# Eight PSUM banks, one written-out order: the same steps of an RWKV attention and squared-ReLU MLP kernel in another sequence

## The chip, the cores and the metric

The kernel runs on one core of a Trainium2 chip. A core has five engines with a queue of instructions each: TensorE (PE: matmuls; its weight loads are listed apart as PEld), VectorE (DVE), ScalarE (ACT), GpSimd (POOL) and SyncE (SP, which here only issues DMAs). The metric is the device time of one execution in microseconds.

## What is computed

A linear attention with a decaying state (4 batches, 8 heads, 768 tokens, head size 48), whose output feeds a two-layer MLP with squared ReLU (384 to 2048 to 384).

```python
def _attn_ref(r, k, v, w, u) -> np.ndarray:
    B, H, S, D = r.shape
    state = np.zeros((B, H, D, D), dtype=np.float32)
...
    for t in range(S):
...
        cur = np.einsum('bhd,bhe->bhde', u[None] * kt, vt)
        y[:, :, t] = np.einsum('bhd,bhde->bhe', rt, state + cur)
        state = w[None, :, :, None] * state + np.einsum('bhd,bhe->bhde', kt, vt)
...
def _moe_ref(x, w_in, w_out) -> np.ndarray:
    h = np.maximum(x @ w_in, 0.0)
    return (h * h @ w_out).astype(np.float32)
```

## The kernel before

The 3072 tokens are cut into 24 units of 128 tokens (`UNITS`: batch and chunk). Within a unit the attention is a masked matrix product, and the 48 x 48 state is carried from chunk to chunk of a batch. The MLP runs on groups of one or two units (`GROUPS`).

Nothing is scheduled by a tool while the kernel is built. The text `ORDER` (line 23) lists all 948 steps. Its entries read `name.indices:engine/slot`: `F1.1.2:P/5` is step F1 of group 1, part 2, on TensorE, with PSUM bank 5. The loop at the end goes through the text, notes the slot as the place of the tile that the step writes, and calls the method of that name of class `Do`. Every engine works through its own steps strictly in the order of the text; between engines, semaphores hold a step back until its inputs are there and its slot is free. The order between entries of different engines in the text therefore means nothing by itself, but a step that waits holds up everything behind it on its engine, and on SP and POOL also the DMAs that are issued behind it.

The steps, with their letters for the engines (A = ACT, D = DVE, G = POOL, P = TensorE, S = SP) and the lines at which the profile lists them:

- Setting up: w, u, wc load the decay vectors; lw takes the logarithm; Z (L564) multiplies an identity by itself for nothing but to occupy TensorE (of n matmuls, n/4 are 512 columns wide, the rest 128); bw (L276) spreads the logarithms over the partitions; Wk (L298) and Wt (L302) make the decay factors; mP and mJ the masks; V (L331) and W (L334) load the quarters of the two MLP matrices, from POOL's queue.
- Loading: lp (L325) loads r, k or v of two units at once for the first four units, ld (L321) of one unit for the others.
- Attention on DVE and POOL: kh (L337) and rh (L340) multiply k and r by their factors; P0 (L343), P1 (L347), du (L350) and dv (L355) make the term with u; vb (L253 on ACT, L255 on DVE or POOL, shared with all plain copies) converts v.
- Transposing k and r: for the first four units TK and TR (L364) with the copies KC and RC; for units 4, 5 and 9 T (L398) with the copy Tc; for the others XB (L404), a DMA transpose.
- Attention on TensorE: Ap (L384) or A (L411), masked into SBUF by Bp (L392) or Bm (L419); Y (L428, L436, L440 for the first four units, L450 and L452 later) makes the output of a unit; U (L463) its contribution to the state.
- State: S0 (L478), ts (L481) and S (L484) update the state of a batch, which Y of the batch's next chunk reads: S.18 writes what Y.22 reads.
- Turning the output round: xs (L475) brings Y out of PSUM, then either X (L489), three transposes on TensorE, with the copy xTc, or xX (L496), a DMA transpose on SP's queue.
- MLP: F1 (L505) is a part of the first product, re (L515 ACT, L517 DVE) its ReLU, sq (L522, L524) the square; F2 (L533) adds a quarter of the second product for a unit, os (L253, L255) copies it out, out (L583, L585) stores it. The last unit, 23, has its second product in two column halves: Fh (L547), oh, outh (L560).

V.2 is the third quarter of the first MLP matrix; F1.0.2, F1.1.2 and all F1 of later groups that fall into that quarter wait for it.

The buffers are fixed in number (`POOLS`); PSUM has eight banks of 128 x 512 float32, used by all TensorE steps:

```python
    banks = [psum.tile([128, 512], FP32, name=f"bank_{j}") for j in range(8)]
```

Of the kernel before, what the change touches and what calls it, by code (L numbers as in the profile page):

```python
# [38 lines left out]
F2.1.2:P/7 P1.5:G du.5:D/0 Bm.5.1:D/2 xs.4:D/4 U.4:P/5 sq.2.0:A/11 sq.2.5:A/12 X.4:P/3 Bm.5.0:D/3 Y.5:P/0 re.2.6:D/1
dv.5:G F2.1.0:P/7 sq.2.3:D/13 F2.3.0:P/6 sq.2.6:D/14 xs.5:D/0 X.5:P/4 F2.0.0:P/1 xTc.5:D/1 xTc.4:A/1 F1.3.1:P/0  # L40
ld.k.6:S/6 re.2.2:D/5 sq.2.2:D/15 re.3.1:D/4 ld.r.6:S/6 P0.6:G/0 F1.3.2:P/4 F1.3.6:P/3 ld.v.6:S/6 vb.6:A/6 U.5:P/2
S0.5:D os.1:A/0 F2.3.2:P/6 F2.3.3:P/6 re.3.2:D/3 re.3.6:A/0 sq.3.6:A/16 rh.6:G/6 F2.3.1:P/6 kh.6:G/6 U.6:P/0
sq.3.2:D/17 ld.r.7:S/7 os.0:D/1 S0.4:D F1.3.0:P/2 F1.3.7:P/7 F2.2.3:P/4 re.3.7:A/2 ld.k.7:S/7 ts.6:D/0 kh.7:G/0
os.3:D/2 rh.7:G/0 re.3.0:A/1 F1.3.3:P/3 sq.3.0:A/18 F2.2.2:P/4 F1.3.4:P/1 re.3.3:A/5 sq.3.3:A/19 F2.2.0:P/4 P0.7:G/2
F2.2.1:P/4 os.2:A/3 out.2:A P1.6:G ld.k.8:S/0 P1.7:D ld.k.9:S/1 ld.v.7:S/7 kh.9:D/1 F2.5.1:P/5 S.3:D ld.r.9:S/0
rh.9:G/1 T.9:P/7 P0.9:D/3 sq.3.1:D/20 ld.r.8:S/1 re.3.4:D/0 XB.7:S/0 du.6:D/1 A.7:P/0/6 du.7:D/2 P1.9:G F1.3.5:P/2
Bm.7.1:D/4 F2.4.1:P/3 Bm.7.0:D/5 rh.8:G/2 ld.v.9:S/0 XB.6:S/6 A.6:P/4/1 Bm.6.0:D/6 F2.4.0:P/3 Bm.6.1:D/7 vb.7:A/7
dv.6:G P0.8:G/4 dv.7:G Y.7:P/6 re.3.5:A/3 du.9:D/3 xs.7:D/1 sq.3.7:A/21 F2.4.3:P/3 sq.3.5:A/22 sq.3.4:A/23 out.1:A
Y.6:P/0 U.7:P/4 F2.4.2:P/3 X.7:P/1 F2.5.2:P/5 xTc.7:A/2 Tc.9:A/1 xs.6:D/2 X.6:P/2 os.4:A/3 xTc.6:D/2 ld.r.11:S/2
rh.11:G/3 ld.k.11:S/2 F2.5.0:P/5 ld.r.10:S/3 F1.4.7:P/6 F2.5.3:P/5 kh.8:D/2 kh.11:G/3 P1.8:G ld.k.10:S/3 ts.7:D/1  # L50
ld.v.8:S/1 rh.10:G/4 kh.10:D/4 vb.9:A/0 re.4.7:D/1 sq.4.7:D/24 os.5:A/0 F1.4.1:P/1 re.4.1:A/5 sq.4.1:A/25 F1.4.4:P/7
F1.4.3:P/0 re.4.4:A/4 S.7:G vb.8:G/1 S.6:D du.8:D/4 dv.8:G F1.4.0:P/3 re.4.0:A/2 U.8:P/2 ts.8:D/1 U.9:P/4 F1.4.2:P/6
re.4.3:A/3 XB.11:S/2 A.11:P/5/1 ts.9:D/0 P0.11:G/1 re.4.2:A/0 sq.4.3:A/26 Bm.11.0:D/0 A.9:P/7/3 Bm.9.0:D/1 P0.10:G/0
# [5 lines left out]
xs.11:D/1 ld.r.13:S/5 rh.13:G/0 kh.13:D/0 F1.5.5:P/7 re.5.3:A/3 sq.5.3:A/0 re.5.5:A/0 ld.k.15:S/6 kh.15:G/6 F1.5.7:P/6
F1.5.1:P/3 re.5.7:A/2 F1.5.2:P/1 vb.12:A/4 X.10:P/0 re.5.1:D/1 X.11:P/7 xTc.11:D/1 F1.5.4:P/6 xTc.10:A/1 ld.r.12:S/6  # L60
P0.12:D/2 P1.12:G re.5.0:A/4 rh.12:G/5 P0.15:D/3 du.12:D/1 P1.15:G ld.r.14:S/7 F1.6.2:P/3 out.5:S ld.v.15:S/6
rh.14:G/1 ld.r.17:S/0 F1.5.6:P/7 re.5.6:D/5 F1.6.0:P/0 F1.6.3:P/5 F2.7.1:P/2 F2.6.2:P/4 rh.17:G/2 F2.7.3:P/2 dv.12:G
sq.5.7:A/3 re.5.4:A/3 P0.13:D/4 P1.13:G sq.5.1:A/1 re.6.2:A/2 XB.13:S/0 ld.k.14:S/7 kh.14:G/1 sq.5.5:A/2 F1.6.7:P/7
# [10 lines left out]
rh.16:G/4 dv.15:G F1.7.3:P/0 xs.15:D/0 os.8:D/0 dv.14:G xs.14:D/4 kh.16:D/4 F1.7.7:P/7 S.15:D ld.r.19:S/2 re.7.7:A/5
ld.r.21:S/3 F1.7.0:P/2 rh.19:G/5 sq.7.7:A/16 F1.7.1:P/4 re.7.1:A/2 xX.15:S/0 F1.7.5:P/1 F1.7.2:P/3 P0.16:D/2 P1.16:G
X.14:P/5 xTc.14:D/0 ld.r.18:S/6 re.7.2:A/1 sq.7.1:A/21 re.7.5:A/4 P0.21:D/4 kh.19:G/5 P1.21:G ld.v.17:S/0 re.7.3:A/3
sq.7.2:A/4 P0.19:D/3 S.12:D rh.21:G/3 out.9:S sq.7.3:A/25 ld.k.18:S/4 U.14:P/7 ts.14:D/1 F2.11.2:P/6 F2.11.3:P/6
F1.8.6:P/4 re.8.6:D/0 P0.18:D/1 vb.17:A/0 re.7.0:A/5 XB.16:S/2 out.8:A F1.8.3:P/5 F1.8.7:P/3 re.8.7:D/2 sq.7.5:A/26
# [557 lines left out]
```

## Time and profile before

| | us |
|---|---|
| median of 3 timed runs | 171.6 |
| lowest and highest | 170.86, 171.61 |
| the profiled execution | 169.91 |
| its span, first to last instruction | 168.2 |
| TensorE busy in it | 161.5 |
| DVE busy | 135.3 |
| POOL busy | 104.3 |
| ACT busy | 100.8 |

The profile is of one execution. Rows of instructions have a start, a duration, the engine, the line, output and inputs and a count; a bracket tells how long the engine was idle before and what ended that. Rows of the chain of waits have a start, a duration and what the end of the kernel waited for in that time. A matmul's end is modelled, so busy time of TensorE can hold a stall.

### The profile page before, as it was taken

How to read it: one execution, taken by the hardware profiler on the slowest of the kernel's cores; microseconds unless marked ns; L12 is line 12 of the kernel's file. 1: busy time of each engine (PE TensorE's matmuls, PEld its weight loads, DVE VectorE, ACT ScalarE, POOL GpSimd, SP SyncE). 2: the span in 40 equal slices, each digit the busy share in tenths (PEclk: the TensorE clock that was granted, in tenths of full speed). 3: DMA queues.
4: the chain of work that ended last, by engine and by line, in shares of the span. 5: the costliest groups of instructions: out<-in, count | busy, mean ns of one | idle time of the engine just before them, and what ended most of it. 6: DMA issues, size and time to landing. Idle time of an engine off the chain costs nothing.

```text
span 168.2 us, 4593 instructions
## 1 busy us (share of the span) xinstructions
PE 161.5 (96%) x1821; PEld 122.8 (73%) x1821; DVE 135.3 (80%) x255; ACT 100.8 (60%) x191; POOL 104.3 (62%) x123
## 2 busy tenths in 40 slices
...
GB/s 135 313 248 201 207 213 199 183 197 205 169 200 143 101 195 168 209 181 189 111 171 186 202 106 224 221 147 145 166 122 211 266 147 94 74 23 51 91 102 90
DMA packets 97575, 27.77 MB, mean 165 GB/s; under 512 B 91789, under 2 KB 97554, under 8 KB 97554
## 3 DMA queue, kind: packets, MB, share of 16 engines
...
q0 software_dynamic: 2720, 3.15, 10.7%
...
q8 instruction: 14, 0.23, 0.6%
...
## 4 chain that ended last, share of the span: by engine, by line
PE 94%; ACT 3%; issue 1%; POOL 0%; POOLq 0%
PE bank L505 38%; PE bank L533 36%; PE bank L411 3%; PE bank L564 2%; PE bank L452 2%; PE bank L450 2%; ACT rkT L253 2%; PE bank L489 2%; PE bank L463 2%; PE bank L547 2%; PE bank L440 1%; ACT vb L253 1%; PE bank L276 1%; PE bank L398 1%; PE bank L428 1%
## 5 line engine op out<-in xcount | busy, mean ns | idle before, releaser
L505 PE MATMUL bank<-xT,W 128*128 128x256 bf16 (+1 forms) x672 | 69.1, 257 | 0.0
L533 PE MATMUL bank<-W,hq 128*128 128x384 bf16 x368 | 67.5, 326 | 0.0
L505 PEld LDWEIGHTS <-W 128*128 128x128 bf16 x672 | 56.7, 98 | 7.6 <-DVE xT L255 0.4
L515 ACT ACTIVATE hr<-bank 128x512 bf16<-128x512 f32 x68 | 38.9, 596 | 27.1 <-PE bank L505 26.4
L533 PEld LDWEIGHTS <-hq 128*128 128x128 bf16 x368 | 33.9, 98 | 18.8
L522 ACT ACTIVATE hq<-hr 128x512 bf16<-128x512 bf16 x66 | 39.4, 630 | 8.3 <-DVE hr L517 7.4
L419 DVE TENSOR_TENSOR Bm<-bank,maskJT 128x512 bf16<-128x512 f32 x40 | 25.5, 681 | 3.0 <-PE bank L411 2.8
L347 POOL TENSOR_TENSOR P<-P,ub 128x384 f32<-128x384 f32 x20 | 21.3, 1067 | 7.1 <-DVE P L343 6.3
L355 POOL TENSOR_TENSOR dv<-ldv,du 128x384 f32<-128x384 f32 (+1 forms) x18 | 15.2, 850 | 16.1 <-DVE du L350 16.1
L340 POOL TENSOR_TENSOR rk<-ldr,Wt 128x384 bf16<-128x384 f32 x17 | 19.4, 1142 | 2.8 <-DMA ldr<-in_r_dram 2.8
L517 DVE TENSOR_SCALAR hr<-bank 128x512 bf16<-128x512 f32 x28 | 19.0, 683 | 1.7 <-PE bank L505 1.6
L524 DVE TENSOR_TENSOR hq<-hr 128x512 bf16<-128x512 bf16 x30 | 17.0, 579 | 2.4 <-ACT hr L515 2.0
L484 POOL TENSOR_TENSOR S0W<-ts,WLm 128x384 bf16<-128x384 f32 x11 | 12.2, 1105 | 10.5 <-DVE ts L481 9.8
L253 ACT COPY os<-bank 128x384 f32<-128x384 f32 (+1 forms) x13 | 6.1, 467 | 13.6 <-PE bank L533 8.8
L350 DVE TENSOR_REDUCE du<-P 128x8 f32<-128x384 f32 x24 | 12.8, 543 | 1.2 <-POOL P L347 1.2
L337 POOL TENSOR_TENSOR rk<-ldk,Wk 128x384 bf16<-128x384 f32 x12 | 13.1, 1099 | 0.0
L343 POOL TENSOR_TENSOR P<-ldr,ldk 128x384 f32<-128x384 f32 x11 | 11.8, 1077 | 1.0 <-DMA ldk<-in_k_dram 0.5
L475 DVE TENSOR_TENSOR xs<-bank,dv 128x384 bf16<-128x384 f32 x20 | 10.7, 549 | 1.8 <-issue 1.6
L343 DVE TENSOR_TENSOR P<-ldr,ldk 128x384 f32<-128x384 f32 x13 | 9.9, 777 | 2.4 <-DMA ldk<-in_k_dram 2.4
L255 DVE COPY os<-bank 128x384 f32<-128x384 f32 (+1 forms) x12 | 6.4, 535 | 6.5 <-PE bank L533 5.7
L481 DVE TENSOR_TENSOR ts<-bank,S0W 128x384 f32<-128x384 f32 x16 | 8.7, 550 | 2.2 <-PE bank L463 1.6
L452 PE MATMUL bank<-vb,Bm 128*128 128x48 bf16 x160 | 9.3, 183 | 0.0
...
## 6 DMA issues: line engine op xcount, KB each, us to landing
...
```

Source lines behind the costliest of these rows:

```text
L337: e.tensor_mul(rk[slot[f"rk{i}"]][:, 1, :, 0:D], loaded("k", i), Do.factor("k", i % 2 if i < PAIRED else 2))
L340: e.tensor_mul(rk[slot[f"rk{i}"]][:, 0, :, 0:D], loaded("r", i), Do.factor("t", i % 2 if i < PAIRED else 2))
L343: e.tensor_mul(P0b[slot[f"P{i}"]], loaded("r", i), loaded("k", i))
L347: e.tensor_mul(t, t, ub)
L355: e.tensor_mul(dv_of(i) if i < PAIRED else dvb[slot[f"dv{i}"]], loaded("v", i), t)
L419: e.tensor_mul(Bmb[slot[f"Bm{i}{h}"]], heads(bank(f"bA{i}{h}"), 128), mask_b)
L505: e.matmul(hp[:, fi, :], W1[f // 4][:, c, 256 * (f // 2 % 2) : 256 * (f // 2 % 2 + 1)].rearrange("p (m j) -> p j m", j=2)[:, f % 2, :], xt ...
L515: e.activation(hr, hp, AF.Relu)
L517: e.tensor_scalar_max(hr, hp, 0.0)
L522: e.activation(hq, hr, AF.Square)
L524: e.tensor_mul(hq, hr, hr)
L533: e.matmul(bank(f"bO{i}")[:, 0:d_model], hqb[slot[f"hq{g},{f // m}"]][:, at : at + L], W2[q][:, f % 4, :], start=(seen[i] == 1 and f % 4 = ...
```

## The change

The text `ORDER` is replaced by another; nothing else in the file differs. All steps stay, apart from these: X.13 with its copy xTc.13 becomes xX.13, and the four Z steps of 15, 20, 12 and 3 matmuls become five of 12, 23, 19, 3 and 10. Many steps change their place in the queue of their engine, slots are numbered anew, and some move to another engine: DVE gets 4 of P1, 6 of rh, 5 of re, 1 of sq and 1 of xTc more, and 2 of kh, 2 of S, 4 of os and 1 of Tc fewer; 5 of vb go from ACT to POOL, and two output stores from ACT's queue to SP's.

Both texts are cut here to the head, the lines that move T.4, T.5, X.13, S.18 and Y.22, and the end.

```diff
--- before.py
+++ after.py
@@ -21,92 +21,93 @@
...
 ORDER = """
-lp.r.0:S/0 w:A u:G tab:A wc.1:A lw:A mP.1:G Z.15:P/0 bw:P/0 mP.0:G Wk.0:A/1 Wk.1:A/2 Wt.0:A/3 Wt.1:A/4 wc.0:A
-lp.k.0:S/0 P0.1:G/0 P0.0:D/1 kh.0:D/0 kh.1:D/1 Z.20:P/5 TK.0:P/5 KC.0:A/0 lp.r.1:S/1 lp.v.0:S/0 shu:D V.0:G rh.0:D/0
-vb.0:A/0 rh.1:D/1 Z.12:P/6 TR.0:P/6 RC.0:A/1 vb.1:A/1 rh.2:D/2 rh.3:D/3 Z.3:P/7 TR.1:P/7 RC.1:A/2 WLcol:A P1.0:G
-P1.1:D V.3:G du.0:D/0 lp.k.1:S/1 V.1:G du.1:D/1 kh.2:D/2 P0.2:G/2 kh.3:D/3 Ap.0.1:P/5/6 Ap.0.0:P/3/4 dv.0:G
-Bp.0.0.0:D/0 TK.1:P/7 Bp.0.1.0:D/1 lp.v.1:S/1 vb.2:A/2 vb.3:A/3 KC.1:A/3 U.1:P/1 Bp.0.1.1:D/2 U.0:P/2 WLm:G
-Bp.0.0.1:D/3 S0.0:D U.3:P/3 U.2:P/5 Ap.1.1:P/7/6 dv.1:G Y.0:P/4 xs.0:A/0 Y.1:P/2 P1.2:G Bp.1.1.1:D/4 du.2:D/2 ts.1:D/0
-V.2:G ld.k.4:S/4 ld.k.5:S/5 Wk.2:A xs.1:A/1 P0.3:G/3 P1.3:G dv.2:G X.0:P/4 xTc.0:D/0 Ap.1.0:P/6/1 Bp.1.0.1:D/5 X.1:P/2
-xTc.1:A/1 F1.0.0:P/4 re.0.0:A/0 F1.0.3:P/1 re.0.3:A/1 F1.1.0:P/2 du.3:D/3 F1.1.3:P/4 Bp.1.0.0:D/6 dv.3:G re.1.0:A/2
-sq.0.3:A/0 Bp.1.1.0:D/7 Y.2:P/1 xs.2:A/2 Wt.2:A W.2:G S0.2:D F1.1.1:P/6 ts.3:D/1 Y.3:P/2 ld.r.4:S/4 xs.3:A/3
-sq.1.0:A/1 F1.0.1:P/7 re.0.1:A/3 X.2:P/1 S.1:D X.3:P/0 F1.1.2:P/5 xTc.3:D/0 rh.4:D/4 xTc.2:A/0 re.1.2:A/4 sq.0.0:A/2
...
-sq.2.7:D/5 P0.4:D/4 F1.2.1:P/7 re.2.1:A/4 sq.2.1:D/6 mJ:G kh.4:G/4 T.4:P/0 sq.1.3:D/7 ld.r.5:S/5 P0.5:D/1 Tc.4:D/4
-sq.0.2:D/8 F1.2.4:P/1 F1.2.0:P/5 re.2.0:A/3 F1.2.5:P/6 re.2.5:A/0 rh.5:G/5 T.5:P/3 F1.2.6:P/4 ld.v.4:S/4 Tc.5:A/5
...
-sq.6.4:A/23 xs.13:D/3 A.14:P/0/2 Bm.14.0:D/0 A.15:P/4/5 Bm.15.0:D/6 Bm.14.1:D/3 F2.10.3:P/7 S.13:G kh.17:G/2 X.13:P/1
-xTc.13:A/2 F2.10.0:P/7 vb.15:A/7 F2.10.2:P/7 Bm.15.1:D/7 F1.7.6:P/0 ld.v.16:S/1 out.7:S re.7.6:A/0 U.15:P/4 os.10:D/1
...
-F1.10.4:P/2 U.18:P/4 P0.23:D/0 F1.10.6:P/7 sq.9.0:A/6 ts.18:D/1 F1.10.2:P/3 ld.v.21:S/7 S.18:G dv.20:D kh.23:G/1
...
-dv.21:G xs.21:D/1 vb.22:G/7 dv.22:G F2.18.3:P/2 re.10.0:D/0 xX.20:S/0 A.22:P/6/3 A.23:P/0/7 os.16:D/3 out.17:A
-sq.10.1:D/16 Bm.22.1:D/3 F2.19.2:P/4 xX.21:S/0 F2.19.3:P/4 sq.10.0:A/20 F2.19.0:P/4 Bm.22.0:D/7 Y.22:P/5 xs.22:D/2
...
-out.20:A F2.22.3:P/2 F2.22.1:P/2 os.22:D/0 out.22:A Fh.23.0.1:P/7 Fh.23.1.1:P/7 Fh.23.3.1:P/7 Fh.23.2.1:P/7
-oh.23.1:D/2 Fh.23.2.0:P/5 Fh.23.1.0:P/5 Fh.23.0.0:P/5 Fh.23.3.0:P/5 oh.23.0:A/1 outh.23.1:S outh.23.0:S
...
+u:G lp.r.0:S/0 w:A tab:A lw:A wc.0:A Z.12:P/0 bw:P/0 Wk.1:A/1 Wk.0:A/2 wc.1:A Wt.1:A/3 lp.k.0:S/0 P0.0:D/0 kh.1:D/0
+Wt.0:A/4 mP.1:G P0.1:G/1 kh.0:D/1 V.0:G Z.23:P/5 TK.0:P/5 shu:D KC.0:A/0 V.3:G rh.1:D/0 P1.1:D rh.0:D/1 Z.19:P/6
+TR.0:P/6 mP.0:G lp.r.1:S/1 rh.3:D/2 rh.2:D/3 Z.3:P/7 TR.1:P/7 lp.v.0:S/0 vb.0:A/0 P1.0:G vb.1:A/1 U.0:P/5 RC.0:A/1
+lp.k.1:S/1 Ap.0.1:P/3/4 kh.2:D/3 Ap.0.0:P/6/2 kh.3:D/2 TK.1:P/1 WLcol:A du.1:D/0 du.0:D/1 RC.1:A/2 Bp.0.0.0:D/0
+Bp.0.1.0:D/1 Bp.0.1.1:D/2 lp.v.1:S/1 vb.2:A/2 vb.3:A/3 Z.10:P/7 U.3:P/7 KC.1:A/3 V.1:G WLm:G Bp.0.0.1:D/3 dv.1:G
+U.2:P/6 U.1:P/3 S0.0:D Ap.1.1:P/4/1 Bp.1.1.0:D/4 dv.0:G Y.0:P/2 xs.0:A/0 ts.1:D/0 Bp.1.1.1:D/5 P0.2:G/2 Y.1:P/5
+X.0:P/4 xTc.0:D/0 Wt.2:A Ap.1.0:P/2/3 P0.3:G/3 P1.3:D P1.2:G du.2:D/2 V.2:G xs.1:A/1 Wk.2:A X.1:P/1 xTc.1:A/1
+F1.0.0:P/4 dv.2:G du.3:D/3 Bp.1.0.0:D/6 F1.0.3:P/5 F1.1.3:P/0 re.1.3:A/0 sq.1.3:A/0 Bp.1.0.1:D/7 S0.2:D F1.1.0:P/1
+re.1.0:A/1 ld.k.4:S/4 ld.r.4:S/4 rh.4:D/4 dv.3:G Y.2:P/2 xs.2:A/2 kh.4:G/4 P0.4:D/4 P1.4:D ts.3:D/1 Y.3:P/0 xs.3:A/3
+re.0.3:A/2 sq.0.3:A/1 F1.1.1:P/3 T.4:P/6 Tc.4:A/4 W.2:G X.3:P/1 du.4:D/4 xTc.3:D/0 X.2:P/2 F1.0.1:P/7 F1.1.2:P/0
+xTc.2:D/0 F1.2.4:P/5 re.2.4:A/3 W.1:G ld.r.5:S/5 W.3:G F1.2.5:P/6 re.2.5:A/4 rh.5:G/5 ld.k.5:S/5 kh.5:D/5 re.1.2:D/5
+re.1.1:D/0 sq.1.1:D/2 sq.1.2:D/3 sq.2.4:D/4 sq.1.0:D/5 re.0.1:A/2 T.5:P/1 Tc.5:A/5 re.0.0:A/0 F1.0.2:P/2 F1.2.0:P/5
+P0.5:G/1 sq.2.5:D/6 P1.5:D F1.2.6:P/6 F1.2.3:P/0 re.2.0:A/5 re.2.3:A/3 A.4:P/3/7 A.5:P/1/4 F1.2.7:P/5 F1.2.2:P/0 mJ:G
...
+dv.15:D XB.14:S/1 A.14:P/2/7 Bm.15.1:D/0 Bm.15.0:D/3 Bm.14.1:D/6 F2.10.3:P/5 xX.12:S/2 xX.13:S/2 du.14:D/2 dv.14:D
...
+sq.10.4:A/21 re.10.0:A/0 Y.21:P/5 xs.21:D/0 du.23:D/0 F2.19.3:P/1 re.10.3:A/4 sq.10.3:A/14 vb.22:G/6 F2.18.3:P/3
+sq.10.5:D/17 F2.17.2:P/7 F2.18.2:P/3 os.16:A/2 F2.18.1:P/3 P0.22:G/2 P1.22:D du.22:D/4 dv.22:G A.22:P/6/5 Bm.22.0:D/6
+Bm.22.1:D/7 A.23:P/4/2 vb.23:A/4 F2.19.2:P/1 Bm.23.0:D/0 F2.19.1:P/1 sq.10.1:A/23 Bm.23.1:D/3 sq.10.0:D/25 S.18:G
+Y.22:P/6 xs.22:D/3 xX.21:S/0 F1.11.5:P/5 out.15:A xX.22:S/1 F1.11.3:P/4 re.11.3:A/3 F1.11.7:P/2 F1.11.0:P/6
...
+Fh.23.3.1:P/3 F1.13.1:P/2 re.13.1:A/5 out.21:S F1.13.2:P/6 F2.22.2:P/0 re.13.2:D/1 sq.13.1:D/10 sq.12.0:A/8
...
+F2.22.1:P/0 Fh.23.2.1:P/3 oh.23.1:D/1 outh.23.1:S F2.22.0:P/0 os.22:D/2 Fh.23.3.0:P/1 Fh.23.1.0:P/1 Fh.23.2.0:P/1
+out.22:S oh.23.0:A/0 outh.23.0:S
 """
```

More of the change, by code (lines that the diff above doesn't have):

```diff
@@ L39 @@
[L39 to L53, printed above, removed]
@@ L59 @@
[L59 to L63, printed above, removed]
@@ L74 @@
[L74 to L78, printed above, removed]
@@ new lines @@
+du.5:D/0 U.4:P/1 S0.4:D re.0.2:A/4 sq.0.2:A/9 F2.3.2:P/3 Y.4:P/5 xs.4:D/4 W.0:G ld.v.5:S/5 F2.1.2:P/4 F2.1.1:P/4
+vb.5:G/5 Y.5:P/1 X.4:P/2 F2.1.3:P/4 dv.5:G xs.5:D/0 X.5:P/5 re.2.2:A/0 ld.k.6:S/6 re.2.6:A/1 sq.2.6:A/10 F2.3.3:P/3
+ld.r.6:S/6 F2.0.2:P/1 xTc.4:D/1 xTc.5:D/1 F1.3.7:P/0 F1.3.0:P/6 ld.v.6:S/6 F1.3.1:P/2 re.2.1:A/4 sq.2.1:D/11
+sq.2.0:D/12 F1.3.5:P/5 rh.6:D/6 S.3:G S.1:G kh.6:G/6 P0.6:D/0 P1.6:G ld.k.7:S/7 ld.r.7:S/7 du.6:D/1 re.3.7:A/1
+sq.2.3:A/13 vb.6:A/6 P0.7:D/2 re.3.5:A/4 sq.3.5:A/14 rh.7:G/2 F2.1.0:P/4 U.5:P/7 F1.3.6:P/0 F1.3.2:P/5 re.3.6:D/5
@@ new lines @@
+F2.4.1:P/4 F2.5.1:P/6 U.7:P/0 ld.r.8:S/2 P1.9:G rh.8:G/1 dv.6:G Y.7:P/7 xs.7:D/1 Bm.6.0:D/7 ts.7:D/0 sq.3.4:A/23
+out.1:A out.2:A T.9:P/5 Tc.9:A/1 F2.4.3:P/4 F2.4.2:P/4 Y.6:P/1 xs.6:D/3 ld.k.11:S/2 kh.11:G/0 ld.k.10:S/3 P0.8:G/4
+X.7:P/2 F2.5.0:P/6 X.6:P/7 xTc.6:D/2 F2.5.2:P/6 ld.r.10:S/3 kh.10:D/4 xTc.7:A/2 F1.4.7:P/3 re.4.7:A/1 F1.4.0:P/0
+re.4.0:D/2 S.7:G F1.4.2:P/5 re.4.2:D/0 P1.8:G du.8:D/3 ld.v.9:S/0 vb.9:A/0 U.9:P/1 ts.9:D/0 rh.10:G/4 S.6:G du.9:D/4
+os.5:A/0 sq.4.7:A/24 F1.4.3:P/7 re.4.3:A/5 os.4:A/3 sq.4.0:D/25 F1.4.4:P/2 re.4.4:A/3 ld.v.8:S/1 vb.8:G/1 P0.11:G/1
@@ new lines @@
+U.8:P/3 ts.8:D/1 F1.4.1:P/0 re.4.1:A/4 sq.4.2:A/26 XB.11:S/2 A.11:P/5/1 Bm.11.0:D/0 A.9:P/6/7 Bm.9.1:D/2 F1.4.6:P/4
+Bm.9.0:D/1 F1.4.5:P/2 sq.4.1:A/27 F2.6.0:P/3 XB.8:S/3 A.8:P/0/5 Bm.11.1:D/3 Bm.8.1:D/4 Bm.8.0:D/5 XB.10:S/4 A.10:P/7/6
+Bm.10.0:D/6 Y.9:P/1 sq.4.3:A/3 F2.6.1:P/3 re.4.6:A/1 sq.4.6:A/2 F2.6.3:P/3 Y.8:P/5 ld.v.11:S/2 dv.9:G xs.9:D/2
+F2.7.0:P/0 X.9:P/7 dv.8:G xs.8:D/4 X.8:P/4 re.4.5:A/2 vb.11:A/2 Y.11:P/1 sq.4.4:A/0 sq.4.5:A/9 F2.6.2:P/3 out.5:S
+ld.v.10:S/3 ld.r.12:S/4 P1.11:G P0.10:G/0 P1.10:G xTc.9:A/0 vb.10:G/3 xTc.8:A/0 Bm.10.1:D/7 Y.10:P/5 F1.5.1:P/2
@@ new lines @@
+ld.r.13:S/5 ld.k.12:S/4 F1.5.4:P/7 re.5.4:A/0 F1.5.7:P/4 F1.5.5:P/6 du.10:D/0 dv.10:G du.11:D/2 dv.11:G rh.13:G/5
+rh.12:G/6 ld.k.15:S/5 ld.k.13:S/6 F1.5.0:P/7 xs.11:D/0 P0.12:D/2 xs.10:D/1 F2.7.3:P/0 P0.13:D/4 re.5.7:D/4 X.10:P/1
+F1.5.3:P/5 xTc.10:A/1 os.6:A/0 re.5.3:A/5 sq.5.3:A/5 kh.12:D/6 kh.13:G/5 ld.r.15:S/6 P0.15:G/3 re.5.5:D/1 re.5.0:D/3
+sq.5.0:A/1 F1.5.2:P/4 S.8:G X.11:P/1 xTc.11:D/1 re.5.1:D/2 re.5.2:D/5 sq.5.2:D/11 F2.7.2:P/0 U.10:P/3 F1.5.6:P/5
+ts.10:D/1 F1.6.0:P/6 F1.6.2:P/7 sq.5.7:A/12 F1.6.3:P/1 F1.6.7:P/2 F1.6.5:P/4 P1.12:G ld.v.14:S/4 vb.14:A/4 re.5.6:A/3
@@ new lines @@
+ld.r.17:S/0 ld.v.15:S/6 vb.15:G/6 sq.6.2:A/10 F2.10.1:P/5 F2.11.1:P/1 ts.13:D/0 U.11:P/4 ld.k.17:S/0 out.4:S P1.14:G
+XB.15:S/6 F2.9.3:P/7 sq.6.7:A/13 ts.11:D/1 re.6.4:A/5 F2.9.2:P/7 P0.17:G/1 sq.6.0:A/20 out.0:S P1.17:G ld.r.19:S/2
+S.11:G rh.19:G/1 du.15:D/3 kh.17:G/4 rh.17:G/4 sq.6.6:A/21 sq.6.1:A/22 F2.11.0:P/1 sq.6.4:A/16 os.9:A/3 A.15:P/6/4
+dv.15:D XB.14:S/1 A.14:P/2/7 Bm.15.1:D/0 Bm.15.0:D/3 Bm.14.1:D/6 F2.10.3:P/5 xX.12:S/2 xX.13:S/2 du.14:D/2 dv.14:D
+ld.k.19:S/1 os.7:A/1 out.7:S F2.10.0:P/5 sq.6.5:A/18 out.6:A F2.11.2:P/1 U.12:P/4 Y.15:P/6 xs.15:D/4 F2.10.2:P/5
```

84 lines of the change are left out of this document (42 added, 42 removed).

## The prediction

> **What bounds the kernel now.** I read the page's busy table first, then three stretches of the span (busy time by engine), then the chain of waits in order of time, and last the rows of the steps that the change moves.
>
> ```profile
> span 168.2 us, 4593 instructions
> PE 161.5 (96%) x1821; PEld 122.8 (73%) x1821; DVE 135.3 (80%) x255; ACT 100.8 (60%) x191; POOL 104.3 (62%) x123
> ...
> PE bank L505 38%; PE bank L533 36%; PE bank L411 3%; PE bank L564 2%; PE bank L452 2%; PE bank L450 2%; ACT rkT L253 2%; PE bank L489 2%; PE bank L463 2%; PE bank L547 2%; PE bank L440 1%; ACT vb L253 1%; PE bank L276 1%; PE bank L398 1%; PE bank L428 1%
> ```
> ```profile
> 1.98:17.00 15.02, 13.39 (x195) 8.78 (x196) 12.86 (x35) 10.31 (x19) 13.31 (x21) 1.00 1.18 253
> 17.00:165.10 148.10, 148.07 (x1629) 114.00 (x1627) 121.57 (x217) 89.55 (x171) 89.98 (x94) 1.00 0.83 161
> 165.10:168.20 3.10, 0.00 (x0) 0.00 (x0) 0.00 (x0) 0.32 (x1) 0.00 (x0) 1.00 0.18 62
> ```
>
> The second fence is the result of the reading: stretch and length, then busy PE, weight loads, DVE, ACT, POOL, the granted clock and the DMA share. From 17.0 us, where the first F1 matmuls start, to 165.1 us TensorE is busy for 148.07 of 148.10 us at a granted clock of 1.00. So the time is a head of 17.0, a body of 148.1 that is TensorE's own work, and an end of 3.1 us. But a busy matmul row may hide a stall, so its pace is checked on the chain:
>
> ```profile
> 124.11 2.62 PE bank L505 x24
> 155.94 6.50 PE bank L533 x40
> ```
>
> 24 F1 matmuls of 256 columns in 2.62 us are 2345 columns per us; 40 F2 matmuls of 384 are 2363. All of F1 is 24 units x 16 chunks x 3 x 128 = 147,456 columns, 62.9 us at that pace; F2 with its split halves is 24 x 16 x 384, as many, 62.4 us; together 125.3. The page's chain, its last line in the first fence, gives L505 38%, L533 36%, L547 2%; 76% of 168.2 is 127.8. So some 2.5 us at most could be stalls inside busy F1 and F2, and the rest of the body is Y, A, U, X and T, which no order removes. The Trainium skill, Perfetto Trace Analysis, section Identifying the Most-Contended Engine, says that matmul busy time is a bad measure of the distance to the roofline and weight-load busy time a better one; by it 73% would leave 45 us of headroom. The two pace rows contradict that here, and what they leave open is the 2.5 us.
>
> **The change part by part.** It permutes the order of each engine's queue, moves some elementwise steps between engines, and gives the PSUM banks new numbers; both orders use banks 0 to 7. Three things alter what TensorE must do. The four warm-up groups Z (15, 20, 12, 3 matmuls) become five (12, 23, 19, 3, 10). X.13, three transposes on TensorE, becomes xX.13, a DMA transpose. And the last output stores move. Otherwise only waits can change.
>
> *Head.* These rows are the chain that sets 17.0 us, with DVE and POOL rows beside it:
>
> ```profile
> 5.15 2.13 PE bank L564 x5
> 7.28 0.87 PE bank L364 x8
> 8.17 1.01 ACT rkT L253
> 10.40 0.52 ACT vb L253
> 12.99 0.92 ACT rkT L253
> 13.96 0.42 PE bank L384 x16
> 17.02 2.72 PE bank L505 x48
> ```
> ```profile
> 5.62 0.56 DVE L343 TENSOR_TENSOR P<-ldr,ldk 128x384 f32<-128x384 f32 x1 [1.73 <-DMA ldk<-in_k_dram]
> 10.56 0.64 PE L384 MATMUL bank<-rkT,rkT 48*64 48x128 bf16 x32 [0.67 <-ACT rkT L253]
> 11.67 2.48 DVE L392 TENSOR_TENSOR Bm<-bank,maskP 128x512 bf16<-128x512 f32 x4
> ```
>
> The wide Z matmuls cost 2.13/5 = 0.43 us each here, so 0.11 for one of 128 columns. The first Z loses three narrow ones (-0.32), the second gains three (+0.32): TK.0 again starts at 7.28, and KC.0, the first copy, at 8.17. DVE starts at 5.62 when k lands, in both orders; up to the first Bp it then runs the same 13 steps in another order, so Bp could again start at 11.67. ACT runs the same nine steps from 8.17 on, so KC.1 (12.99 + 0.92) ends at 13.91 and Ap.1.1, which waits for it, starts at 13.96 as before. What moves inside is RC.0: vb.1 now goes ahead of it, so it ends one vb later, 0.5 us. With that the two Ap.0 groups end at 10.56 + 0.64 + 0.5 = 11.70 instead of 11.20, still within 0.1 of DVE's 11.67; Bp ends at 14.25, and Y.0 behind Ap.1.1 (13.96 + 0.42 = 14.38) hides it. The longer third Z (19) fills the time in which TR.0 waits for rh.0, which now has P1.1 ahead of it on DVE, and Z.10 lies under the same wait for KC.1. Head: 0. Bounds: -0.3 to +0.5, the Z term one way, and the vb step if its cover, Ap.1.1's wait, is gone.
>
> *V.2, the one load that is issued later.* On POOL it goes from ahead of P0.3 to behind P0.2, P0.3 and P1.2:
>
> ```profile
> 13.06 0.83 POOL L355 TENSOR_TENSOR dv<-ldv,du 128x384 bf16<-128x384 f32 x1
> 13.85 1.00 POOL L347 TENSOR_TENSOR P<-P,ub 128x384 f32<-128x384 f32 x1
> 14.80 0.80 POOL L331 DMA_DIRECT2D W<-in_moe_w_in_dram  x1
> ```
> ```profile
> L331 POOL DMA_DIRECT2D W<-in_moe_w_in_dram x2: 775/790/804, 8.8 to 9.6; - x2
> DMA to landing us min/median/max: 7.2/8.5/9.8
> DMA to landing us min/median/max: 7.7/7.7/7.7
> ```
>
> Up to the second dv POOL has the same work in both orders, but for P0.2 (about 1.0) in the place of one mask; so it ends at 13.9 again, three multiplications of 1.0 follow, and V.2 is issued at 16.9 instead of 14.8. TensorE needs it at F1.1.2. From 19.74 (17.02 + 2.72) the new order puts Y.2, Y.3, F1.1.1, T.4, X.3, X.2 and F1.0.1 ahead of it; by the rows
>
> ```profile
> 20.02 0.50 PE bank L440 x16
> 20.53 0.78 PE bank L505 x12
> 23.14 0.34 PE bank L489 x6
> 26.13 0.45 PE bank L398 x8
> ```
>
> that is 2 x 0.8 (0.28 more than the L440 row for what precedes it) + 2 x 0.78 + 0.45 + 0.34 = 3.95, hence 23.7. The second and third V loads, issued at 8.8 and 9.6, landed at 16.0 and 19.4, and V.2 (14.8 + 7.7) at 22.5: 3.1 to 3.4 us apart although the issues are 0.8 and 5.2 apart. So they come one after another, and V.2 waits for its predecessor, not for its issue. A V.2 issued at 16.9, 2.5 us before V.1 lands, should land near 22.5 as well. Cost 0; bounds: 0, and +0.9 if it takes its 7.7 us from the issue (24.6 against 23.7).
>
> *X.13 to xX.13.* X.13 is half of the 0.34 us row of six above: -0.17, between -0.33 (alone, nothing beside it) and 0. Its cover: the two transposes of group 7 must land before F1.7.4.
>
> ```profile
> 88.53 1.22 SPq L496 DMA_TRANSPOSE xT<-xs  x1
> DMA to landing us min/median/max: 2.3/2.5/4.5
> 93.28 0.66 PE bank L505 x6
> ```
>
> The second follows the first by 1.22 on SP's queue: 88.53 + 1.22 + 2.5 = 92.3, against a first F1.7 near 93.3. A landing of 4.5 would cost 1.0.
>
> *Steps between engines.* DVE takes four P1, six rh, five re, an sq and an xTc, and gives two kh, two S, four os and a Tc: eight steps more. At the 0.62 of a Bp (2.48/4) that is 5.0 us, 140.3 of 168.2 or 83% instead of 80%, taken from POOL and ACT.
>
> ```profile
> 120.00:130.00 10.00, 10.00 (x95) 8.57 (x93) 9.90 (x18) 6.31 (x12) 6.04 (x6) 1.00 0.99 164
> ```
>
> DVE is already full for 9.90 of 10 us here, and TensorE does not miss any of it. So 83% alone costs nothing: cost 0, with TensorE's own work as the cover; without it, a late step costs up to its own length, and the largest that I find is priced below with S.18.
>
> *End.* out.22 now goes out on SP between the two half stores of unit 23.
>
> ```profile
> 162.44 2.65 PE bank L547 x32
> 164.23 1.56 SPq L560 DMA_DIRECT2D out_dram<-os  x2
> 165.11 0.32 ACT L253 COPY os<-bank 128x192 f32<-128x192 f32 x1 [3.46 <-PE bank L547]
> ```
>
> Three Fh groups of 0.33 (2.65/8) follow F2.22.0. os.22 (0.55) is done 0.4 us before TensorE ends, its issue takes about 0.35, and the last store waits for oh.23.0, 0.36 after TensorE's end, anyway. I take +0.1, between 0 and +0.5 for its 192 KB ahead of the last 96.
>
> Sum: 0 + 0 - 0.17 + 0 + 0.1 = -0.1 us on a profiled execution of 169.91 us (span 168.2 and 1.7 around it), 169.8. The three timed runs had a median of 171.6, 1.7 above that execution; with the same distance the forecast is 171.5.
>
> **The rivals.** 0.5% (0.86 us) is about what a measurement of this kernel tells from no change.
>
> *Slower: V.2 comes late.* Place: F1.1.2, which blocks every matmul behind it on TensorE. It decides when V.2 lands after 23.7, 6.8 us from its issue. For it: a DMA share of 1.18 in the head, so every transfer queues, and landings of 7.2 to 9.8 us in the three V rows. Against it: the even spacing. Price +0.9 with 7.7 us and +3.0 with the 9.8 of the third V; I take 1.5: 173.0.
>
> *Slower: S.18 gates Y.22.* S.18 moves from long before to POOL's very last step, behind dv.22.
>
> ```profile
> L355 POOL TENSOR_TENSOR dv<-ldv,du 128x384 f32<-128x384 f32 (+1 forms) x18 | 15.2, 850 | 16.1 <-DVE du L350 16.1
> L484 POOL TENSOR_TENSOR S0W<-ts,WLm 128x384 bf16<-128x384 f32 x11 | 12.2, 1105 | 10.5 <-DVE ts L481 9.8
> L350 DVE TENSOR_REDUCE du<-P 128x8 f32<-128x384 f32 x24 | 12.8, 543 | 1.2 <-POOL P L347 1.2
> ...
> 90.50 0.55 PE bank L411 x16
> ```
>
> From Y.21's end DVE runs xs.21, du.23, sq.10.5, P1.22, du.22 (five of about 0.55) and POOL dv.22 and S.18 (0.85 + 1.1): 4.7 us. TensorE has seven F2 groups (0.65) and two A (0.55 together) between Y.21 and Y.22: 5.1. Margin 0.4, less the handovers; it decides once POOL's two or DVE's five lose that, and costs up to 1.1. With a second thin margin like the transposes' (1.0) it makes 172.8.
>
> *Faster.* The new order would have to remove stalls hidden in busy rows, at most 2.5 us, or those of the timed runs, which take 1.7 us more than the profiled one. For it: that difference. Against it: TensorE's 148.07 of 148.10. Half of the 1.7: 170.6. The page of the Trainium skill named above would put the room for it in TensorE's queue as well.
>
> *Nothing is changed in effect*, because banks, pools and work are the same and TensorE's body is its own work: that is the forecast itself.
>
> **How the numbers follow.** Forecast 0.44. V.2 late 0.18, S.18 or the transposes 0.18, faster 0.20. So faster 0.20, same 0.44, slower 0.36. The forecast's own range is 170.8 to 172.3 (head -0.3 to +0.5, X.13, the end, and the spread of the runs shown, 170.86 to 171.61). The whole range reaches down to the faster case with its spread, 170.3, and up to V.2 at 1.5 with the head's 0.5, 173.5.
>
> **What would show it.** First F1 matmul at 17.0 and TensorE without a gap behind it: right. V.2: a gap ahead of F1.1.2 near 23.7 whose releaser is the W load. S.18: TensorE's Y.22 near 141 waiting for POOL L484. xX.13: F1.7.4 near 93 waiting for xT. The end: 3.1 us from the last matmul to the end. A head past 17.5, or a body whose F1 and F2 paces differ from 2345 and 2363, makes the prediction wrong.

## The result and the profile after

| | before | after |
|---|---|---|
| median, us | 171.2 (14 runs, 169.81 to 171.74) | 169.65 (14 runs, 169.44 to 176.78) |
| profiled execution, us | 169.91 | 169.46 |
| its span, us | 168.2 | 167.8 |

The ratio of after to before is 0.9928, 95% interval 0.9900 to 0.9956: 0.7% faster. Runs that were disturbed are left out of the ratio. The forecast was 171.5, in a range of 170.3 to 173.5. Yet the two profiled executions differ by only 0.45 us. First the page of after, then its three stretches (columns as in the prediction, with GB/s last; the line numbers of after are one higher, since its `ORDER` has one line more):

```profile
span 167.8 us, 4600 instructions
PE 162.1 (97%) x1826; PEld 122.4 (73%) x1826; DVE 137.6 (82%) x263; ACT 97.5 (58%) x183; POOL 99.8 (59%) x122
```
```profile
1.98:16.76 14.78, 14.30 (x202) 8.60 (x203) 12.99 (x35) 10.62 (x20) 12.43 (x20) 1.00 1.17 254
16.76:164.66 147.90, 147.80 (x1628) 113.80 (x1625) 123.71 (x225) 85.92 (x163) 86.32 (x94) 1.00 0.82 161
164.66:167.80 3.14, 0.01 (x1) 0.00 (x0) 0.00 (x0) 0.32 (x1) 0.00 (x0) 0.94 0.26 94
```

The head is 16.76 us instead of 17.0, the body 147.90 instead of 148.10, the end 3.14 instead of 3.10. Next, the rows for the steps that were costed: from the chain of waits, the first Bp group and 24 F1 matmuls; from the timeline, V.2's issue on POOL, the two DMA transposes xX.12 and xX.13, and the first F1 matmuls of group 7.

```profile
11.56 2.49 DVE Bm L393 x4
119.58 2.62 PE bank L506 x24
```
```profile
16.46 0.80 POOL L332 DMA_DIRECT2D W<-in_moe_w_in_dram  x1
86.32 2.95 SPq L497 DMA_TRANSPOSE xT<-xs  x2
93.69 2.13 PE L506 MATMUL bank<-xT,W 128*128 128x256 bf16 x18
```

Bp starts at 11.56 (11.67 in the prediction's fence), F1 has the same pace, V.2 is issued at 16.46 (16.9 forecast) and nothing waits for it, and F1.7 starts at 93.69 with no idle time in front of it. Read profile against profile, the sum had the right sign and a small size: -0.45 measured, -0.1 forecast. The body's -0.20 lies beside the -0.17 put down to xX.13, but that may be luck: the recorded execution loses 0.17 us at X.5 as well (below), and without this loss the body would be shorter by as much. What the forecast missed is that the usual execution of before isn't the profiled one.

### The profile page after: what moved, and what is told of

The parts are those of the page before. It is cut to its first block, busy times and chain, and to the rows that moved or that the text cites. A ratio compares the mean times of both kernels' runs of the same rounds, so it can differ in the third digit from the quotient of the medians.

```text
span 167.8 us, 4600 instructions
## 1 busy us (share of the span) xinstructions
PE 162.1 (97%) x1826; PEld 122.4 (73%) x1826; DVE 137.6 (82%) x263; ACT 97.5 (58%) x183; POOL 99.8 (59%) x122
## 4 chain that ended last, share of the span: by engine, by line
PE 82%; DVE 8%; issue 4%; DMA 2%; SPq 0%; ACT 0%; DVEq 0%
PE bank L506 36%; PE bank L534 34%; PE bank L412 3%; DMA ldk<-in_k_dram 2%; PE bank L453 2%; DVE Bm L393 2%; PE bank L451 2%; PE bank L464 2%; DVE rk L341 1%; PE bank L490 1%; DVE P L344 1%; DVE rk L338 1%; DVE P L348 1%; DVE du L351 1%; PE bank L441 1%
## 5 line engine op out<-in xcount | busy, mean ns | idle before, releaser
L516 ACT ACTIVATE hr<-bank 128x512 bf16<-128x512 f32 x63 | 36.3, 596 | 33.1 <-PE bank L506 31.4
L518 DVE TENSOR_SCALAR hr<-bank 128x512 bf16<-128x512 f32 x33 | 22.0, 683 | 5.8 <-PE bank L506 5.0
L338 POOL TENSOR_TENSOR rk<-ldk,Wk 128x384 bf16<-128x384 f32 x14 | 15.3, 1096 | 10.0 <-DMA ldk<-in_k_dram 10.0
L356 POOL TENSOR_TENSOR dv<-ldv,du 128x384 f32<-128x384 f32 (+1 forms) x18 | 16.0, 894 | 7.4 <-DVE du L351 7.3
L254 ACT COPY os<-bank 128x384 f32<-128x384 f32 (+1 forms) x17 | 7.8, 468 | 20.0 <-PE bank L534 12.5
L348 POOL TENSOR_TENSOR P<-P,ub 128x384 f32<-128x384 f32 x16 | 16.5, 1032 | 3.8 <-DVE P L344 3.5
L485 POOL TENSOR_TENSOR S0W<-ts,WLm 128x384 bf16<-128x384 f32 x13 | 13.5, 1041 | 8.4 <-DVE ts L482 8.3
L525 DVE TENSOR_TENSOR hq<-hr 128x512 bf16<-128x512 bf16 x31 | 14.4, 488 | 0.9 <-ACT hr L516 0.7
L341 POOL TENSOR_TENSOR rk<-ldr,Wt 128x384 bf16<-128x384 f32 x11 | 12.4, 1135 | 4.1 <-DMA ldr<-in_r_dram 4.1
L254 ACT COPY rkT<-bank 128x1024 bf16<-128x1024 bf16 x7 | 7.1, 1008 | 3.2 <-DVE Bm L420 2.4
```

What stands on the lines that cost most here:

```text
L254: e.copy(o, a)
L338: e.tensor_mul(rk[slot[f"rk{i}"]][:, 1, :, 0:D], loaded("k", i), Do.factor("k", i % 2 if i < PAIRED else 2))
L348: e.tensor_mul(t, t, ub)
L356: e.tensor_mul(dv_of(i) if i < PAIRED else dvb[slot[f"dv{i}"]], loaded("v", i), t)
L516: e.activation(hr, hp, AF.Relu)
L518: e.tensor_scalar_max(hr, hp, 0.0)
```

## The experiments

### Is it the head, or the order behind it?

Unchanged; then the order before with the five Z groups, `Z.12 Z.23 Z.19 Z.3` and a `Z.10` behind TK.1; then the new order with the four old ones.

> The kernel before, unchanged, to see an execution that is not its fastest. Its 14 timed runs had a median of 171.2 us and the profiled one took 169.91. Theory H (the head: in most executions TensorE's matmuls stay slow for longer after the start, and the profiled one was a lucky one): time 171.2, ratio 1.00, and where this profile is of a 171 us execution, the first F1 or the body behind it is 1 to 1.7 us later with longer matmuls near 8 to 20 us. Theory L (loads: in most executions some load lands late): the same time, but a gap on TensorE with a DMA or POOL step as its releaser in the body.

> The order before with only the warm-up matmuls of the order after: Z of 12, 23, 19, 3 in the same four places and a Z of 10 behind TK.1. Theory H (the gain is the longer third Z and the added one, which keep TensorE busy from 8 to 13 us): 169.6 to 170.0, ratio 0.99 to 0.993. Theory L (the gain is in loads and waits of the body): 171.2 or slightly more (the added Z delays Ap.1.1 by up to 0.3), ratio 1.00.

> The order after with the warm-up matmuls of the order before: Z of 15, 20, 12, 3, the Z of 10 taken out. Theory H: back to 171.2, ratio 1.00. Theory L: 169.6 as the changed kernel, ratio 0.992.

Measured: unchanged 170.94 (12 runs) beside 170.74; e2 170.85, ratio 1.0008 (0.9984 to 1.0032); e3 169.99, ratio 0.9945 (0.9913 to 0.9978). So the Z groups don't make the gain, and the order without them keeps most of it. But they do something. Each run is listed with its granted clock. In these three kernels it was 0.99 or less in 11 of the 41 unchanged runs and in 4 of 12 of e3, and in none of 12 of e2. The profile of the unchanged order fell on such an execution; its stretches of one microsecond:

```profile
16.00:17.00 1.00, 1.00 (x23) 0.63 (x20) 0.43 (x2) 0.48 (x1) 0.92 (x2) 0.50 1.20 194
17.00:18.00 1.00, 1.00 (x14) 1.00 (x11) 0.89 (x2) 0.47 (x1) 1.00 (x2) 0.50 1.22 195
18.00:19.00 1.00, 1.00 (x13) 1.00 (x11) 1.00 (x3) 0.20 (x2) 0.94 (x2) 0.50 1.29 235
19.00:20.00 1.00, 1.00 (x17) 1.00 (x16) 0.97 (x3) 0.56 (x2) 1.00 (x3) 0.80 1.21 192
```

The granted clock, the third column from the end, halves for three microseconds and 0.4 of the next, (1 - 0.80)/0.50. TensorE reads 1.00 busy all the while. Only the counts and durations tell: 14 and 13 matmuls in the second and third of these microseconds, where the recorded execution of before has 21 and 22, and 1.02 us more for the first 48 F1 matmuls. First the row of the unchanged order, then that of the recorded execution:

```profile
17.29 3.86 PE L505 MATMUL bank<-xT,W 128*128 128x128 bf16 x48
```
```profile
16.90 2.84 PE L505 MATMUL bank<-xT,W 128*128 128x128 bf16 x48
```

3.4 us at half clock take 1% off the mean clock, (3.4 x 0.5)/168, which is the clock of 0.99 listed for the run. The profiles of e3 and e8 fell on such executions too: half clock from 15.9 to 19.3 us and from 16.6 to 20.0. Over all experiments, the unchanged order's runs at a clock of 0.99 lie at 171.6 to 172.0; those at 0.98, which two such windows would give by the same sum (no profile shows one), at 172.85 to 173.6; those at 0.997 or more have a median of 170.6 to 170.7 beside each experiment.

The slow stretch that theory H looked for is there, then. The same profile shows a second thing, as does that of e2, of the kind that theory L looked for but with a DVE step as its releaser: X.5 waits for xs.5. The first row is from the timeline of the unchanged order, the second from e2's list of TensorE's waits (total, times, longest):

```profile
39.43 0.34 PE L489 MATMUL bank<-identity,xs 128*128 128x128 bf16 x3 [0.47 <-DVE xs L475]
```
```profile
PE bank L489 <- DVE xs L475: 0.6, 1, 0.6
```

### Is it X.5, behind two squares?

In DVE's queue of the order before, two squares stand in front of xs.5. e4 moves xs.5 ahead of them, e5 does so with the five Z groups, e6 does the opposite to the new order, e7 profiles the unchanged one again.

```diff
 e4, e5
-dv.5:G F2.1.0:P/7 sq.2.3:D/13 F2.3.0:P/6 sq.2.6:D/14 xs.5:D/0 X.5:P/4 ...
+dv.5:G xs.5:D/0 F2.1.0:P/7 sq.2.3:D/13 F2.3.0:P/6 sq.2.6:D/14 X.5:P/4 ...
 e6, from after
-... dv.5:G xs.5:D/0 X.5:P/5 ... F1.3.1:P/2 re.2.1:A/4 sq.2.1:D/11 sq.2.0:D/12 F1.3.5:P/5 ...
+... dv.5:G re.2.1:A/4 sq.2.1:D/11 sq.2.0:D/12 xs.5:D/0 X.5:P/5 ... F1.3.1:P/2 F1.3.5:P/5 ...
```

> The order before, with the one step xs.5 put ahead of the two DVE squares sq.2.3 and sq.2.6 that stood in front of it. Theory L1 (most of the gain comes from one stall in the body, X.5 waiting for xs.5 behind the two squares, 0.47 and 0.60 us in the two looks that had it): X.5 no longer waits, and the median falls by about 0.5 us, to 170.2-170.4 beside 170.7-170.9. Rival L2 (the gain is spread over many waits of 0.1 to 0.3 us): X.5's wait goes too, but the median falls by 0.2 at most, since TensorE then waits a little further on. Rival H (the clock in the head sets the median): no difference, 170.7-170.9.

> The order before with both edits: the five Z groups of the new order, and xs.5 ahead of the two squares. L1: 170.2-170.4, with no run at a granted clock under 0.997. L2: 170.6-170.8, no run under 0.997 either. If the head and the one stall together are all of the gain: 169.6-169.9, as the new order.

> The new order, with its two DVE squares sq.2.1 and sq.2.0 put in front of xs.5, as two squares stand in the order before. In the new order only X.4 and one F2 group (0.17 + 0.65 us) lie between Y.5 and X.5, so xs.5 (0.55) behind two squares (1.5 to 2.1 us) makes X.5 wait 1.2 to 1.9 us. L1 and L2 (what TensorE waits in the body is lost for good): 170.8-171.6 beside 169.65. Rival A (a wait there is absorbed, because TensorE makes it up from waits further on): under 0.5 us more, at most 170.1.

> Unchanged order before, one more look. L1: X.5 waits 0.4-0.6 us for xs.5 and the span is 168.7-169.2 at a clock of 1.00. L2: a span of about 169 with several waits of 0.1 to 0.3 us and no single larger one. H: a granted clock under 0.995 in the head and a span over 169.5.

Measured: e4 170.67, ratio 0.9964 (0.9928 to 1.0000), its runs at a full clock at a median of 170.66, as before; e5 170.72, 0.9995 (0.9972 to 1.0018); e6 170.68, 0.9998 (0.9969 to 1.0026); e7 170.61 at a span of 168.9 and a clock of 1.00, so a usual run without the clock's part. Its timeline shows the place: DVE, POOL, then TensorE.

```profile
35.77 2.12 DVE L524 TENSOR_TENSOR hq<-hr 128x512 bf16<-128x512 bf16 x2
37.81 0.55 DVE L475 TENSOR_TENSOR xs<-bank,dv 128x384 bf16<-128x384 f32 x1
```
```profile
35.47 1.00 POOL L340 TENSOR_TENSOR rk<-ldr,Wt 128x384 bf16<-128x384 f32 x1
36.42 2.31 POOL L337 TENSOR_TENSOR rk<-ldk,Wk 128x384 bf16<-128x384 f32 x2
```
```profile
36.07 1.46 PE L533 MATMUL bank<-W,hq 128*128 128x384 bf16 x8
38.41 0.34 PE L489 MATMUL bank<-identity,xs 128*128 128x128 bf16 x3 [0.88 <-DVE xs L475]
```

Two squares take 2.12 us, xs.5 ends at 38.36, and X.5 starts at 38.41. The same rows of the recorded execution of before:

```profile
35.47 1.57 DVE L524 TENSOR_TENSOR hq<-hr 128x512 bf16<-128x512 bf16 x2
36.96 0.55 DVE L475 TENSOR_TENSOR xs<-bank,dv 128x384 bf16<-128x384 f32 x1
```
```profile
36.09 1.46 PE L533 MATMUL bank<-W,hq 128*128 128x384 bf16 x8
37.56 0.34 PE L489 MATMUL bank<-identity,xs 128*128 128x128 bf16 x3
```

There the squares took 0.55 us less, X.5 started 0.85 earlier, and no wait is listed. It had no margin even so: xs.5 ended at 37.51 and X.5 started at 37.56. Of the 0.85 us, 0.7 remain at the end (span 168.2 against 168.9). That is how the recorded execution differs from the usual one.

e4 and e5 brought nothing because the stall moved on one step. xs.5 is early, but xTc.5 comes behind the same squares on DVE, and F1.3.1 waits for it. From the timeline of e4:

```profile
37.52 2.22 DVE L524 TENSOR_TENSOR hq<-hr 128x512 bf16<-128x512 bf16 x2
39.66 0.34 DVE L255 COPY xT<-bank 128x384 bf16<-128x384 bf16 x1
```
```profile
40.06 2.14 PE L505 MATMUL bank<-xT,W 128*128 128x256 bf16 x18 [1.01 <-DVE xT L255]
```

My L2 had foreseen that in general, not the place. e6 is the reverse test, and the new order loses its gain by it (170.68 against 169.65). The wait that its profile lists is 0.74 us, less than the 1.2 to 1.9 expected, and the rest of the 1.0 wasn't traced:

```profile
35.97 0.34 PE L490 MATMUL bank<-identity,xs 128*128 128x128 bf16 x3 [0.74 <-DVE xs L476]
```

### Both consumers free of the squares

e8 and e9 put the squares behind xTc.5, without and with the five Z groups. e10 and e11 leave them in place and give them to ACT, with and without the five Z groups.

```diff
 e8, e9
-... sq.2.3:D/13 F2.3.0:P/6 sq.2.6:D/14 xs.5:D/0 X.5:P/4 F2.0.0:P/1 xTc.5:D/1 xTc.4:A/1 ...
+... F2.3.0:P/6 xs.5:D/0 X.5:P/4 F2.0.0:P/1 xTc.5:D/1 sq.2.3:D/13 sq.2.6:D/14 xTc.4:A/1 ...
 e10, e11
-... sq.2.3:D/13 F2.3.0:P/6 sq.2.6:D/14 ...
+... sq.2.3:A/13 F2.3.0:P/6 sq.2.6:A/14 ...
```

> The order before, with both squares sq.2.3 and sq.2.6 moved on DVE from ahead of xs.5 to behind xTc.5, so that neither X.5 nor F1.3.1 has a square in front of what it waits for. Theory L1 (two squares of 1.0 to 1.1 us each in front of TensorE's next input are most of the gain): no wait of TensorE between 35 and 42 us, and a median 0.6 to 0.9 lower, 169.9-170.3 beside 170.7-170.9; runs with a granted clock under 0.995 still occur. Rival L2 (each such stall only moves on to the next step on DVE): a wait of 0.5 us or more at another step before 50 us, and a median of 170.4-170.8.

> The same edit, and the five Z groups of the new order. L1 with the clock as a separate matter: 169.8-170.2, no run with a granted clock under 0.997, highest run under 170.8. L2: 170.4-170.8. If head and squares are all of the gain, the new order's 169.65 within 0.3.

> The five Z groups, and the two squares stay at their place but run on ACT (0.63 us each there, ACT is busy for only 1.9 of the 6 us). L1: as e9, 169.8-170.2, since what counts is that DVE has no slow square in front of xs.5 and xTc.5. L2 or a cause in xs.5 and xTc.5 themselves: 170.4-170.8.

> The order before with one edit only: sq.2.3 and sq.2.6 run on ACT; the four Z groups stay. Theory (two separate causes: the squares set the usual time, the Z groups only how often the clock drops): the runs at a granted clock of 0.997 or more lie at 169.6-170.1, as with the five Z groups; a quarter or so of all runs has a clock of 0.99 or less and lies 1 to 3.5 us higher. Rival (the Z groups also shorten the usual run): all runs above 170.2.

| | median, us | ratio to before, 95% | runs under a clock of 0.997 |
|---|---|---|---|
| e8 | 170.54 | 0.9999 (0.9966 to 1.0032) | 5 of 12 |
| e9 | 170.01 | 0.9962 (0.9938 to 0.9985) | 0 of 12 |
| e10 | 169.68 | 0.9938 (0.9912 to 0.9964) | 0 of 7 |
| e11 | 169.55 | 0.9914 (0.9882 to 0.9946) | 0 of 6 |

As a whole e8 missed the 169.9 to 170.3 expected, but its seven runs at a full clock have a median of 169.98, so squares and clock can be told apart: the squares move the usual run, the Z groups the share of runs with the clock halved. e8 and e9 stay 0.3 to 0.4 us above e10 and e11. In e8's profile a moved square still takes 1.22 us, and TensorE waits 0.68 us at 42.61 for a ReLU that stands behind it on DVE; e9's lists no such wait, so its 0.3 stays open. e11 is the clearest. It changes two letters in the text, nothing else, and the order before takes the new order's time. Six runs without a halved clock don't show that e11 is free of it: over all kernels with the four old Z groups 51 of 182 runs were under 0.997, with the five new ones 3 of 81.

### Why a square takes 1.06 us there and 0.42 elsewhere

The profile e7 holds the answer. Squares, and Bm, which reads one input from PSUM, with the shortest, median and longest duration in ns:

```profile
L524 DVE TENSOR_TENSOR hq<-hr x30: 408/426/1216, 25.6 to 157.8; 128x512 bf16<-128x512 bf16 x30
L419 DVE TENSOR_TENSOR Bm<-bank,maskJT x40: 675/681/692, 31.9 to 145.3; 128x512 bf16<-128x512 f32 x40
```

Of these two, the squares spread, by a factor of three. Two of them, the POOL rows first, then DVE's:

```profile
28.99 1.01 POOL L347 TENSOR_TENSOR P<-P,ub 128x384 f32<-128x384 f32 x1 [3.03 <-DVE P L343]
124.80 1.00 POOL L347 TENSOR_TENSOR P<-P,ub 128x384 f32<-128x384 f32 x1
```
```profile
29.43 0.85 DVE L524 TENSOR_TENSOR hq<-hr 128x512 bf16<-128x512 bf16 x1
124.99 1.09 DVE L524 TENSOR_TENSOR hq<-hr 128x512 bf16<-128x512 bf16 x1
```

The POOL instruction that runs at the start of the square ends at 30.00 and at 125.80; the squares end at 30.28 and 126.08, 0.28 us behind both. The median is 0.43. All 30 squares of e7 fit this: the 14 that start while a POOL instruction runs end 0.279 to 0.284 us behind its end, and the other 16 take 0.408 to 0.426, also the four during which a POOL instruction starts. It is thus not a share of a bandwidth but a block by the one instruction in progress. The Trainium skill, SBUF — State Buffer, section Who interferes with whom, says that a DVE instruction with two SBUF inputs contends with a GpSimd instruction that reads SBUF, that the lock on the shared port pair is exclusive, and that issue order decides who blocks. These rows agree. So does Bm, with its one SBUF input, at 0.675 to 0.692 beside POOL or not. And the squares aren't alone: rh takes 0.60 to 1.26 us on DVE where both its inputs are in SBUF, and 0.54 to 0.55 where its factor is still in PSUM, beside POOL in both cases. To test it, e13 leaves the squares where they are and takes POOL's work away beside them:

```diff
-... xTc.4:A/1 F1.3.1:P/0 ld.k.6:S/6 re.2.2:D/5 sq.2.2:D/15 re.3.1:D/4 ld.r.6:S/6 P0.6:G/0 ...
+... xTc.4:A/1 F1.3.1:P/0 ld.k.6:S/6 ld.r.6:S/6 P0.6:D/0 P1.6:G re.2.2:D/5 sq.2.2:D/15 re.3.1:D/4 ...
...
-... out.2:A P1.6:G ld.k.8:S/0 ...
+... out.2:A ld.k.8:S/0 ...
```

> The order before with its squares in place, but P0.6 on DVE behind xTc.5 instead of on POOL, and P1.6 next on POOL, so that POOL has nothing to do between dv.5 and P0.6, while the squares run. Theory (a square with both inputs in SBUF waits until the POOL instruction that runs at its start has ended, and then takes 0.28 us; alone it takes 0.42): the two squares take 0.7-0.85 us together instead of 2.1, X.5 does not wait, and the runs at a granted clock of 0.997 or more lie at 169.5-170.2. Rival (the squares are slow at this place for another reason, the DMA load or ACT's and TensorE's traffic): 1.8-2.2 us for the two, X.5 waits 0.5-0.9, and 170.4-170.9.

Measured: 169.60, ratio 0.9948 (0.9914 to 0.9982); its nine runs at a full clock lie at 169.49 to 169.64, the other three at 171.02 to 171.09. DVE, POOL and TensorE at the same place:

```profile
35.88 0.75 DVE L524 TENSOR_TENSOR hq<-hr 128x512 bf16<-128x512 bf16 x2
36.55 0.55 DVE L475 TENSOR_TENSOR xs<-bank,dv 128x384 bf16<-128x384 f32 x1
```
```profile
38.73 1.00 POOL L347 TENSOR_TENSOR P<-P,ub 128x384 f32<-128x384 f32 x1 [4.06 <-DVE P L343]
```
```profile
36.16 1.46 PE L533 MATMUL bank<-W,hq 128*128 128x384 bf16 x8
37.46 0.33 PE L489 MATMUL bank<-identity,xs 128*128 128x128 bf16 x3
```

With POOL idle the two squares take 0.75 us, and X.5 follows the start of its two F2 groups by 1.30 instead of 2.34 in e7. So TensorE got back 1.04 us, and the span fell from 168.9 to 167.9. In the recorded execution the distance is 1.47: it had lost 0.17 without a listed wait, because matmul ends are modelled.

### X.13 as a DMA transpose, alone in the old order

e12 adds xX.13 to e10.

```diff
-... X.13:P/1
-xTc.13:A/2 ...
+xX.13:S/2 ...
```

> The order before with the five Z groups, the two squares on ACT, and X.13 with its copy replaced by the DMA transpose xX.13 on SP's queue behind F2.10.3. Theory: TensorE has three transposes less (0.17 us), nothing else: 169.4-169.7, at or 0.2 below the new order's 169.65. Rival (the DMA transpose lands too late for F1.7.4 here): a wait of TensorE on xT between 80 and 100 us and 169.9 or more.

Measured: 171.70, ratio 1.0047 (1.0022 to 1.0072), 2.0 us above e10, where at most 169.7 was expected. From its waits of TensorE (total, times, longest) and from SP's queue:

```profile
PE bank L505 <- DMA xT<-xs: 0.8, 1, 0.8
PE bank L505 <- DVE Bm L419: 0.7, 1, 0.7
PE bank L533 <- DVE hr L517: 0.4, 1, 0.4
```
```profile
88.17 4.21 SPq L496 DMA_TRANSPOSE xT<-xs  x2
```

The pair of transposes is on SP's queue until 92.4, against 89.3 in the new order (86.32 + 2.95), while F1.7 wants its input at about the same time. 92.4 - 1.2 + 2.5 (one issue, one landing) is 93.7, when the waiting F1.7 starts. The 0.7 listed under Bm is that wait by this reckoning. So the step is worth its 0.17 us only where xs.12 and xs.13 come early enough. The 0.8 is a wait of F1.8 at 102.42 us for a later transpose on the same queue. The three waits are 1.9 of the 2.0 us; how the first one brings on the other two wasn't tried.

## Why the prediction was wrong

- **The step that failed** is the last of the sum: "The three timed runs had a median of 171.6, 1.7 above that execution; with the same distance the forecast is 171.5." That distance was no constant around the kernel but stalls that the profiled execution lacked: 0.7 us from X.5, and 1.0 more (171.6 against 170.6) in executions with the clock halved once. Two of the three timed runs, 171.6 and 171.61, lie where such runs lie; their own clocks aren't on record. The new order removes the first and makes the second rare. The chance of 0.20 and the half of 1.7 for *faster* (170.6) named the stalls of the timed runs, without saying what they were, and sized their removal too low. What would show the prediction wrong was a late head or another pace of F1 and F2; neither came, because these signs look at the body of one execution and not at the distance that was added to it.
- **TensorE-bound body, F1 and F2 pace:** held for the recorded execution, even there but for the 0.17 us at X.5. It wasn't true of the usual one.
- **Head 0, bounds -0.3 to +0.5:** measured -0.24 (16.76 against 17.0), inside.
- **V.2 at no cost:** held; issued at 16.46, and nothing waits for it. That rival fell.
- **S.18 and the transposes:** no wait of TensorE on either in the profile of after. Where the transposes are late, as in e12, they cost even more than the price of 1.0. The 172.8 of this rival doesn't follow from its parts: 1.1 and 1.0 above 171.5 are 173.6.
- **xX.13 -0.17 and the end +0.1:** no run resolves them alone in the new order; 3.14 against 3.10 at the end fits.
- **Steps between engines at no cost:** the size was right for the eight steps more on DVE (82% busy), but they were priced at one duration, 0.62. A square costs 0.42 or up to 1.22, by what POOL does beside it, and the new order's pair at this place stands behind both copies.
